# A fused attention and feed-forward kernel: the first block's attention by head halves, narrow dummy matmuls, and m-tiles in column pieces

## Chip, cores and metric

The kernel runs on one core of one Trainium2 chip. The metric is the device time of one execution in microseconds (us). Besides the timed runs there is one profiled execution, from which all views of the trace come.

## The reference

For each of 8 batches and 8 heads, a sequence of 576 tokens is cut into 9 chunks of 64 tokens, and softmax attention is done inside each chunk (head dimension 64). The heads are put side by side, which gives x of 4608 x 512, and x goes through a feed-forward layer with 2048 inner features and a swish with one beta per feature.

```python
def _attn_ref(q, k, v):                      # q, k, v: 8, 8, 576, 64
    scores = scale * np.matmul(q_c, k_c.transpose(0, 1, 2, 4, 3))   # chunks of 64
    scores = scores - np.max(scores, axis=-1, keepdims=True)
    attn = np.exp(scores)
    attn = attn / (np.sum(attn, axis=-1, keepdims=True) + 1e-09)
    return np.matmul(attn, v_c)

def _moe_ref(x, w_in, w_out, beta):          # x: 4608, 512
    h = x @ w_in                             # 512 x 2048
    g = h * (1.0 / (1.0 + np.exp(-beta * h)))
    return g @ w_out                         # 2048 x 512
```

## The kernel before

**Blocks.** The 4608 tokens are cut into nine blocks of 512 (`BLK`). Each block goes through attention (scores, exponential, P·V, normalization, transpose to the tile `xt`), then through L1 (x times w_in, silu, giving the tile `gt`) and L2 (`gt` times w_out, stored). L1 of a block is 16 m-tiles of 128 inner features; an m-tile is four matmuls of 128x128x512 (one for each quarter n of the 512 model columns) in one PSUM tile `hps`. From block 2 on, and in L2 from block 1 on, fewer products are used, with sums and differences of the operands; block 0 uses the plain products (`L1_first`, `L2_plain`). The code writes the order of all work by hand; each engine runs its instructions in that order. The waits between engines follow from the tiles that are read and written.

**Attention.** A group g is four chunks of all eight heads, i a pair of chunks: a block of 512 tokens has two groups and four pairs. The heads come in two halves, z = 0 and 1, of four heads each. q and k of a batch are loaded as two such halves for batch 0 (`split=True`), and each half is transposed on VectorE (`emit_T`, L135). `emit_sc(g)` makes the scores of both halves (L167) in a pair of PSUM tiles (`sc0` and `sc1`, or two of the pool `ps_p`, or the tile `x`) and then exponentials on ScalarE (L176). `emit_pv(i)` multiplies by V (L197); V has a column of ones, so that the sum of the exponentials comes with it. VectorE divides (a reciprocal and a multiplication, L209 to L214), once for the whole tile where the target is `x`, or once for each of two tiles. `emit_xp(i)` transposes the pair on TensorE (L232) and a copy on ScalarE or VectorE brings 128 columns of `xt` to SBUF.

**The head.** TensorE starts with 14 dummy matmuls on zeros, 512 columns wide (`emit_idle`, L244; their result is not read). Then come, in TensorE's order: half 0 of the scores of group 0, ten dummies, half 1 of group 0 and all of group 1, six dummies, P·V of pairs 0 and 1, four dummies, the transpose of pair 0, P·V of pair 2, two dummies, and `L1_first`. `L1_first` works the first four m-tiles in parts of 128 columns, each as soon as the columns of `xt` and the part of w_in are there, first with n = 0 and 2 (half 0 of the heads), then with n = 1 and 3. The m-tiles 4 to 15 follow at full width (`emit_m`).

**Loads.** POOL issues the loads of the inputs in a fixed order: q and k of batch 0 by halves, V of batch 0 in four loads (two for each half of the heads), w_in in five, w_out 0 to 7 in two, q and k of batch 1, w_out 8 to 11, V of batch 1 in four, w_out 12 to 15 in two, q and k of batch 2. beta comes over SP's queue. w_out is scaled by 1/beta (`binv`) after it has landed, on VectorE or ScalarE (`scale_w_out`, L122 and L126).

**L2 of block 0.** `L2_plain(0)` is a list of 20 units; a unit takes rows kk of w_out for one quarter t of the block: units 0 to 7 take kk 0 to 7, units 8 to 11 kk 8 to 11, units 12 to 15 kk 12 and 13, units 16 to 19 kk 14 and 15. Ahead of some units, hooks do the attention of block 1: scores of groups 2 and 3 ahead of unit 8, `emit_pv(4)` ahead of unit 11, `emit_pv(5)` ahead of unit 12, and so on. Block 1's L1 (`L1_plain`) already does its first five m-tiles in pieces of 128 columns and the sixth in two of 256.

Of the kernel before, what the change touches and what calls it, by code (L numbers as in the profile page):

```python
# [8 lines left out]
FP32 = mybir.dt.float32  # L9
FP16 = mybir.dt.float16  # L10
ACTF = mybir.ActivationFunctionType
ALU = mybir.AluOpType
# [3 lines left out]
def kernel(  # L16
# [74 lines left out]
                    in_=src[b].rearrange("(z a) (t r) d -> (a t) z (r d)", z=2, r=RUN)[:, zs],  # L91
                )

    def load_v(b):
        t = vbuf[b % NV]
        for z in range(2):
            for hp in range(2):
                h0 = 4 * z + 2 * hp
                nc.gpsimd.dma_start(  # L99
                    out=t[64 * hp:64 * hp + 64, 2 * z:2 * z + 2, :, 0:D].rearrange(  # L100
                        "p s c d -> p (s c) d"),
                    in_=v[b, h0:h0 + 2].rearrange("s (c p) d -> p (s c) d", p=CH),
                )
# [39 lines left out]
        return [lambda z=z, w=w: emit_T(b, z, w) for z in range(2) for w in range(2)]  # L143

    et_t = {}

    def emit_sc(g, where="s", between=None):
        if where == "x":
            scx = ps_x.tile([128, 2, 2, 4, CH], FP32, tag="x", name="scx")
            sc = [scx[:, 0], scx[:, 1]]  # L150
        else:
            sc = [
                ps_p.tile([128, 2, 4, CH], FP32, tag="p", name=f"scp{s}") if where == "p"
                else ps_s.tile([128, 2, 4, CH], FP32, tag=f"sc{s}", name=f"sc{s}")
                for s in range(2)
            ]
        for z in range(2):
            if z and between:
                between()
            for c in range(4):  # L160
                b, cb = divmod(4 * g + c, NCB)
                for e in range(2):
                    for a in range(4):
                        p0, o0 = 32 * a, 64 * (a // 2)
                        kk = kT[b][p0:p0 + 32, z].rearrange("p t r e -> p (t r) e")
                        qq = qT[b][p0:p0 + 32, z].rearrange("p t r e -> p (t r) e")
                        nc.tensor.matmul(  # L167
                            out=sc[a % 2][o0:o0 + 64, z, c, :],
                            lhsT=kk[:, cb * CH:(cb + 1) * CH, e],
                            rhs=qq[:, cb * CH:(cb + 1) * CH, e],  # L170
                            start=(e == 0),
                            stop=(e == 1),
                        )
        et = et_t[g] = et_p.tile([128, 2, 2, 4, CH], FP16, tag="et", name="et")
        for o, i_ in [(et, scx)] if where == "x" else [(et[:, s], sc[s]) for s in range(2)]:
            nc.scalar.activation(out=o, in_=i_, func=ACTF.Exp, scale=scale)  # L176

    xt_t = {}

    x16_t = {}  # L180

    def emit_pv(i, where="x", xbar=True):
        g = i // 2
        spare = where != "x"
        if where == "p":
            xs = [ps_p.tile([128, 4, 128], FP32, tag="p", name="xp") for _ in range(2)]
        elif where == "s":
            xs = [ps_s.tile([128, 4, 128], FP32, tag=f"sc{h}", name="xp") for h in range(2)]
        else:
            x = ps_x.tile([128, 2, 4, 128], FP32, tag="x", name="x")  # L190
            xs = [x[:, 0], x[:, 1]]
        for s in range(4):
            z, a2 = s // 2, s % 2
            for hp, cp in ((0, 0), (1, 1), (0, 1), (1, 0)):
                b, cb = divmod(2 * i + cp, NCB)
                p0, o0 = 64 * hp, 64 * cp
                nc.tensor.matmul(  # L197
                    out=xs[hp][o0:o0 + 64, s, 0:D + 1],
                    lhsT=et_t[g][p0:p0 + 64, a2, z, 2 * (i % 2) + cp, :],
                    rhs=vbuf[b % NV][p0:p0 + 64, s, cb, 0:D + 1],  # L200
                )
        rd = rd_p.tile([128, 2, 4, 1], FP32, tag="rd", name="rd")
        x16 = x_p.tile([128, 2, 4, D], FP16, tag="x16", name="x16")
        for xx, rr, yy in (
            [(xs[h], rd[:, h], x16[:, h]) for h in range(2)] if spare else [(x, rd, x16)]
        ):
            shape = [128] + list(yy.shape[1:])
            if spare:
                nc.vector.reciprocal(out=rr, in_=xx[:, :, D:D + 1])  # L209
                src = xx[:, :, 0:D]  # L210
            else:
                nc.vector.reciprocal(out=rr, in_=xx[:, :, :, D:D + 1])
                src = xx[:, :, :, 0:D]
            nc.vector.tensor_tensor(  # L214
                out=yy, in0=src, in1=rr.to_broadcast(shape), op=ALU.mult,
            )
        j, t0 = i // 4, (i % 4) * 128
        if j not in xt_t:
            xt_t[j] = xt_p.tile([128, KDM, BLK], FP16, tag="xt", name="xt")
        xf = x16.rearrange("p e s d -> p (e s d)")  # L220
# [33 lines left out]
    def emit_h(j, m, c0=0, c1=BLK, ns=range(KDM)):  # L254
        if (j, m) not in hps_t:
            hps_t[j, m] = ps_p.tile([128, BLK], FP32, tag="p", name="hps")
        for n in ns:
            e, z = n // 2, n % 2
            nc.tensor.matmul(  # L259
                out=hps_t[j, m][:, c0:c1],  # L260
                lhsT=w_r[m // 4][:, 2 * z + e, m // 2 % 2, m % 2, :],
                rhs=xt_t[j][:, n, c0:c1],
                start=(n == 0 and c0 == 0),
                stop=(n == KDM - 1),
                skip_group_check=True,
            )
# [86 lines left out]
        for i in range(2):  # L353
            silu(m2 + i, dn_, sb["t"][:, i])

    def emit_m(j, m):
        emit_h(j, m)
        emit_g(j, m)

    HT = BLK // 2  # L360
# [178 lines left out]
    def dve(n=1):  # L539
        for _ in range(n):  # L540
            if fill:
                fill.pop(0)()

    def L1_first():
        gt_t[0] = gt_p.tile([128, KFF, BLK], FP16, tag="gt", name="gt")

        def part(t, ns, m_last=False):
            for m in range(4):
                emit_h(0, m, t * 128, (t + 1) * 128, ns)
                if m_last:  # L550
                    emit_g(0, m)

        emit_xp(1)
        part(0, (0, 2))
        part(1, (0, 2))
        emit_pv(3, xbar=False)
        emit_xp(2)
        part(0, (1, 3))
        part(1, (1, 3))
        emit_xp(3, eng=nc.vector)  # L560
        table(ACTF.Silu)
        part(2, (0, 2, 1, 3))
        part(3, (0, 2, 1, 3), True)
        for m in range(4, 6):
            hps_t[0, m] = ps_s.tile([128, BLK], FP32, tag=f"sc{m % 2}", name="hps")
        for m in range(4, KFF):
            emit_m(0, m)

    def L1_plain(j, hooks, pieces={}):
        gt_t[j] = gt_p.tile([128, KFF, BLK], FP16, tag="gt", name="gt")  # L570
        for m in range(KFF):
            hooks.get(m, lambda: None)()
            w = BLK // pieces.get(m, 1)
            for c in range(0, BLK, w):
                emit_h(j, m, c, c + w)
            emit_g(j, m)
# [32 lines left out]
    with tc.manual_schedule():  # L609
# [24 lines left out]
        load_w_out(7, 1)  # L634
        load_qk(2)

        emit_idle(14)
        for f in T_items(0):
            f()
        nc.vector.transpose(  # L640
# [6 lines left out]
        nc.vector.scalar_tensor_tensor(  # L647
            out=beta2, in0=bt, scalar=eps, in1=bm, op0=ALU.subtract, op1=ALU.mult)
        nc.vector.tensor_scalar_add(beta2, beta2, eps)
        nc.vector.reciprocal(out=binv, in_=beta2)  # L650
        emit_sc(0, between=lambda: emit_idle(10))
        emit_sc(1, where="p")
        emit_idle(6)
        emit_pv(0, xbar=False)
        emit_pv(1, where="s", xbar=False)
        d = emit_idle(4)
        emit_xp(0, "p")
        emit_pv(2, xbar=False)
        emit_idle(2, d=d)

        L1_first()
        emit_sw()
        scale_w_out(range(0, 4))
        scale_w_out(range(4, 8))
# [132 lines left out]
```

## Time and profile before

| | us |
|---|---|
| five timed runs, median | 278.06 |
| lowest and highest | 277.27, 278.15 |
| profiled execution, its own time | 278.28 |
| span of the profile, first to last instruction | 276.5 |

| engine | busy us (share of the span) |
|---|---|
| PE (TensorE matmul) | 267.7 (97%) |
| PEld (weight load) | 192.4 (70%) |
| DVE (VectorE) | 215.5 (78%) |
| ACT (ScalarE) | 163.3 (59%) |
| POOL (GpSimd) | 95.6 (35%) |

Where the first stages lie, by the timeline: first dummies from 1.19 to 6.24; first scores at 8.91; first P·V at 15.23; first m-tile matmul at 18.23; the last m-tiles of block 0 end and the first `ops` matmul of L2 follows at 33.69; the first m-tile of block 1 begins at 51.38.

A line of the timeline has the start in us, the time in us, the engine, the line of code, the operation, what it writes and reads, the shape, the number of instructions merged in it and, in brackets, the engine's idle time ahead of it with what ended it. Matmuls are pipelined, so that the duration of one (0.38 us for 512 columns) is longer than the distance from one to the next. In a row of windows, each engine's busy time has its number of instructions behind it; then come the granted clock of TensorE as a fraction of full speed, the share of the DMA engines and the GB/s.

### The profile page before, as it was taken

How to read it: one execution, taken by the hardware profiler on the slowest of the kernel's cores; microseconds unless marked ns; L12 is line 12 of the kernel's file. 1: busy time of each engine (PE TensorE's matmuls, PEld its weight loads, DVE VectorE, ACT ScalarE, POOL GpSimd, SP SyncE). 2: the span in 40 equal slices, each digit the busy share in tenths (PEclk: the TensorE clock that was granted, in tenths of full speed). 3: DMA queues.
4: the chain of work that ended last, by engine and by line, in shares of the span. 5: the costliest groups of instructions: out<-in, count | busy, mean ns of one | idle time of the engine just before them, and what ended most of it. 6: DMA issues, size and time to landing. Idle time of an engine off the chain costs nothing.

```text
span 276.5 us, 8403 instructions
## 1 busy us (share of the span) xinstructions
PE 267.7 (97%) x3612; PEld 192.4 (70%) x3612; DVE 215.5 (78%) x428; ACT 163.3 (59%) x276; POOL 95.6 (35%) x106
## 2 busy tenths in 40 slices
PE   7799999999999999999999999999999999999994
PEld 2356444756886688668866886688668866887684
DVE  2744664888688899889988988898679867996854
ACT  2049736878256854785478547853784478316820
POOL 8733445162107820782078204820311031013100
PEclk9799999999999999999999999999999999999999
DMA  6999999999946964797479342924202320232013
GB/s 100 172 200 211 211 180 207 186 261 197 89 117 138 178 59 116 134 179 63 116 149 176 49 116 79 87 42 116 78 0 59 100 76 0 60 98 76 0 40 115
DMA packets 69654, 32.01 MB, mean 116 GB/s; under 512 B 53745, under 2 KB 63985, under 8 KB 69617
## 3 DMA queue, kind: packets, MB, share of 16 engines
q0 software_dynamic: 45024, 18.35, 55.4%
q1 hardware_dynamic: 24448, 12.99, 17.9%
q8 instruction: 28, 0.46, 0.7%
q10 hardware_dynamic: 144, 0.13, 0.1%
q14 instruction: 10, 0.07, 0.1%
HBM read 36.71 MB, written 9.44 MB: 167 GB/s over the span
## 4 chain that ended last, share of the span: by engine, by line
PE 88%; DMA 5%; DVE 3%; POOL 2%; issue 1%; ACT 0%; DVEq 0%; ACTq 0%; POOLq 0%
PE hps L259 27%; PE oA L414 19%; PE wA L313 9%; PE wX L313 6%; PE oB L414 5%; PE oD L414 5%; PE ops L513 5%; PE oC L414 4%; DMA vb<-in_v_dram 3%; PE x L197 2%; PE scx L167 2%; PE sc L167 2%; DMA xt<-x 2%; PE xps L232 1%; POOL vb L99 1%
## 5 line engine op out<-in xcount | busy, mean ns | idle before, releaser
L259 PE MATMUL hps<-xt,wi 128*128 128x512 f16 (+2 forms) x464 | 85.2, 328 | 0.6 <-issue 0.5
L270 ACT ACTIVATE gt<-hps,beta 128x512 f16<-128x512 f32 x88 | 57.8, 683 | 21.0 <-PE hps L259 20.9
L259 PEld LDWEIGHTS <-wi 128*128 128x128 f16 x464 | 39.4, 98 | 27.1 <-issue 0.7
L414 PEld LDWEIGHTS <-s 128*128 128x128 f16 x496 | 47.6, 98 | 6.2 <-DVE s L374 0.5
L414 PE MATMUL oA<-tw,s 128*128 128x256 f16 x368 | 44.3, 273 | 0.0
L414 PEld LDWEIGHTS <-gt 128*128 128x128 f16 x384 | 36.3, 98 | 6.6
L425 ACT COPY u<-oA 128x512 f32<-128x512 f32 x24 | 14.1, 586 | 41.9 <-PE oA L414 41.9
L321 DVE COPY u<-wA 128x512 f32<-128x512 f32 x42 | 28.6, 682 | 5.0 <-PE wA L313 5.0
L99 POOL DMA_DIRECT2D vb<-in_v_dram x32 | 27.4, 874 | 7.0 <-DMA w_out<-in_moe_w_out_dram 3.2
L344 POOL TENSOR_TENSOR t<-u,w 128x512 f32<-128x512 f32 x14 | 17.8, 1274 | 33.6 <-DVE u L321 33.6
L313 PEld LDWEIGHTS <-sw 128*128 128x128 f16 x224 | 21.9, 98 | 9.5 <-issue 0.8
L483 POOL TENSOR_TENSOR o<-t,o 128x512 f32<-128x512 f32 x7 | 8.9, 1271 | 51.7 <-ACT o L480 42.7
L452 POOL TENSOR_TENSOR w<-u,u 128x512 f32<-128x512 f32 x7 | 9.9, 1412 | 47.2 <-ACT u L425 25.9
L135 DVE STREAM_TRANSPOSE qT<-qu 128x576 f32<-128x576 f32 x16 | 20.0, 1250 | 4.3 <-DMA qu<-in_q_dram 4.2
L135 DVE STREAM_TRANSPOSE kT<-ku 128x576 f32<-128x576 f32 x16 | 19.9, 1244 | 3.7 <-DMA ku<-in_k_dram 3.5
L313 PEld LDWEIGHTS <-wi 128*128 128x128 f16 x168 | 16.4, 98 | 4.9
L607 ACT ACT_TABLE_LOAD x15 | 19.2, 1283 | 0.3
L324 ACT ACTIVATE gt<-c,beta 128x512 f16<-128x512 f32 x28 | 18.7, 716 | 0.2
L372 DVE TENSOR_TENSOR s<-gt 128x512 f16<-128x512 f16 x32 | 17.8, 556 | 0.0
L313 PE MATMUL wA<-xs,sw 128*128 128x256 f16 x112 | 16.8, 273 | 0.6 <-DVE u L321 0.6
L374 DVE TENSOR_TENSOR s<-s,gt 128x512 f16<-128x512 f16 x32 | 15.6, 488 | 1.1
L176 ACT ACTIVATE et<-sc 128x512 f16<-128x512 f32 x18 | 9.7, 596 | 11.1 <-PE sc L167 11.1
(87 smaller groups left out, 407.2 us busy)
## 6 DMA issues: line engine op xcount, KB each, us to landing
out_dram<-osb SPq DMA_DIRECT2D x21, 256.0 KB, 3.6
vb<-in_v_dram POOLq DMA_DIRECT2D x32, 144.0 KB, 8.4
out_dram<-o SPq DMA_DIRECT2D x14, 256.0 KB, 2.2
qu<-in_q_dram POOLq DMA_DIRECT2D x6, 576.0 KB, 7.9
ku<-in_k_dram POOLq DMA_DIRECT2D x6, 576.0 KB, 10.7
wi<-in_moe_w_in_dram POOLq DMA_DIRECT2D x3, 512.0 KB, 12.1
w_out<-in_moe_w_out_dram POOLq DMA_DIRECT2D x3, 512.0 KB, 15.6
qu<-in_q_dram POOLq DMA_DIRECT2D x4, 288.0 KB, 11.3
```

Source lines behind the costliest of these rows:

```text
L99: nc.gpsimd.dma_start(out=t[64 * hp:64 * hp + 64, 2 * z:2 * z + 2, :, 0:D].rearrange("p s c d -> p (s c) d"), in_=v[b, h0:h0 + 2].rearrang ...
L135: nc.vector.transpose(out=dst[b][:, z].rearrange("p t r e -> p (t r e)").bitcast(FP32).rearrange("p (t r) -> p r t", r=RUN), in_=src[b][:, ...
L259: nc.tensor.matmul(out=hps_t[j, m][:, c0:c1], lhsT=w_r[m // 4][:, 2 * z + e, m // 2 % 2, m % 2, :], rhs=xt_t[j][:, n, c0:c1], start=(n == ...
L270: nc.scalar.activation(out=gt_t[j][:, m, :], in_=hps, func=ACTF.Silu, scale=beta2[:, m % 2, m // 2:m // 2 + 1],)
L313: nc.tensor.matmul(out=bank[b][:, i, :], lhsT=a[:, kk, q, i, :], rhs=rhs[:, kk, :], start=(first and i == 0 and kk == 0), stop=(kk == 1), ...
L321: nc.vector.tensor_copy(out=sb[nm], in_=bank[b])
L324: nc.scalar.activation(out=gt_t[j][:, m, cols], in_=src, func=ACTF.Silu, scale=beta2[:, m % 2, m // 2:m // 2 + 1],)
L344: nc.gpsimd.tensor_tensor(out=sb["t"], in0=sb["u3"], in1=sb["w1"], op=ALU.add)
L372: tt(out=s1[:, lo], in0=g[:, lo, dn], in1=g[:, hi, dn], op=ALU.add)
L374: tt(out=s2[:, lo], in0=s1[:, lo], in1=g[:, lo, up], op=ALU.subtract)
L414: nc.tensor.matmul(out=bank[name][:, i, :], lhsT=a[:, kk, i * 128:(i + 1) * 128], rhs=b[:, kk, :], start=(first and i == 0 and n == 0), st ...
L607: nc.scalar.activation(out=warm2, in_=warm, func=func, scale=1.0)
```

## The change

The change does several things at once.

- The first 14 wide dummies become 88 of 32 columns and 10 of 512.
- In the head, the two groups are no longer done one after the other, but the halves of the heads are: scores and exponentials of half 0 for both groups (`head_sc(0)`), seven dummies, half 1 for both groups. P·V (`head_pv`) and the transpose (`head_xp`) work on one group and one half at a time, so that a transposed piece holds 256 columns of two quarters n instead of 128 columns of four. The dummies between are 7, 1, 3 and 1 instead of 10, 6, 4 and 2.
- `L1_first` takes the first four m-tiles in four parts of 256 columns and two n each.
- The m-tiles 4 to 11 of block 0 are done in four pieces of 128 columns.
- The reciprocal for `binv` stands after `L1_first` in VectorE's order.
- `load_v` gets a parameter that no call uses; the normalization moves to a function `normed` without change; `sc_part` is the inner part of the old `emit_sc`.

```diff
+    def sc_part(g, z, sc):
+        for c in range(4):
+            b, cb = divmod(4 * g + c, NCB)
+            for e in range(2):
+                for a in range(4):
...
+                    nc.tensor.matmul(
+                        out=sc[a % 2][o0:o0 + 64, z, c, :],
+                        lhsT=kk[:, cb * CH:(cb + 1) * CH, e],
+                        rhs=qq[:, cb * CH:(cb + 1) * CH, e],
...
-    def emit_m(j, m):
-        emit_h(j, m)
+    def emit_m(j, m, pieces=1):
+        w = BLK // pieces
+        for c in range(0, BLK, w):
+            emit_h(j, m, c, c + w)
         emit_g(j, m)
...
+    def head_sc(z):
+        if z == 0:
+            for g in range(2):
+                sc_h[g] = [
+                    ps_s.tile([128, 2, 4, CH], FP32, tag=f"sc{s}", name=f"sc{s}") if g == 0
+                    else ps_p.tile([128, 2, 4, CH], FP32, tag="p", name=f"scp{s}")
+                    for s in range(2)
+                ]
+                et_t[g] = et_p.tile([128, 2, 2, 4, CH], FP16, tag="et", name="et")
+        for g in range(2):
+            sc_part(g, z, sc_h[g])
+            for s in range(2):
+                nc.scalar.activation(
+                    out=et_t[g][:, s, z], in_=sc_h[g][s][:, z], func=ACTF.Exp, scale=scale)
+
+    def head_pv(g, z, where="x"):
+        if where == "s":
+            xs = [ps_s.tile([128, 4, 128], FP32, tag=f"sc{h}", name="xp") for h in range(2)]
+        else:
+            x = ps_x.tile([128, 2, 4, 128], FP32, tag="x", name="x")
+            xs = [x[:, 0], x[:, 1]]
+        for ti in range(2):
+            for a2 in range(2):
+                for hp, cp in ((0, 0), (1, 1), (0, 1), (1, 0)):
+                    c = 2 * ti + cp
+                    p0, o0 = 64 * hp, 64 * cp
+                    nc.tensor.matmul(
+                        out=xs[hp][o0:o0 + 64, 2 * ti + a2, 0:D + 1],
+                        lhsT=et_t[g][p0:p0 + 64, a2, z, c, :],
+                        rhs=vbuf[0][p0:p0 + 64, 2 * z + a2, 4 * g + c, 0:D + 1],
+                    )
+        x16_t[g, z] = normed(xs, None if where == "s" else x)
+
+    def head_xp(g, z, where, eng=None):
+        xf = x16_t.pop((g, z))
...
+        for kk in range(KDM):
+            nc.tensor.transpose(
+                out=xps[:, kk, :], in_=xf[:, kk * 128:(kk + 1) * 128], identity=ident
+            )
+        dst = xt_t[0].rearrange("p (e z) (i c) -> p z e i c", z=2, c=128)[:, z, :, 2 * g:2 * g + 2]
+        src = xps.rearrange("p (e i) c -> p e i c", e=2)
+        if eng:
+            eng.tensor_copy(out=dst, in_=src)
+        else:
+            nc.scalar.copy(out=dst, in_=src)
...
     def L1_first():
...
-        def part(t, ns, m_last=False):
+        def part(g, z):
             for m in range(4):
-                emit_h(0, m, t * 128, (t + 1) * 128, ns)
-                if m_last:
+                emit_h(0, m, g * 256, (g + 1) * 256, (z, 2 + z))
+                if (g, z) == (1, 1):
                     emit_g(0, m)
 
-        emit_xp(1)
-        part(0, (0, 2))
-        part(1, (0, 2))
-        emit_pv(3, xbar=False)
-        emit_xp(2)
-        part(0, (1, 3))
-        part(1, (1, 3))
-        emit_xp(3, eng=nc.vector)
+        part(0, 0)
+        head_xp(0, 1, "x")
         table(ACTF.Silu)
-        part(2, (0, 2, 1, 3))
-        part(3, (0, 2, 1, 3), True)
+        part(1, 0)
+        head_xp(1, 1, "s1", eng=nc.vector)
+        part(0, 1)
+        part(1, 1)
...
         for m in range(4, KFF):
-            emit_m(0, m)
+            emit_m(0, m, 4 if m < 12 else 1)
...
-        emit_idle(14)
+        d = emit_idle(88, w=32)
+        emit_idle(10, d=d)
...
+        head_sc(0)
+        d = emit_idle(7)
+        head_sc(1)
+        emit_idle(1, d=d)
+        head_pv(0, 0)
+        head_pv(1, 0, "s")
+        emit_idle(3, d=d)
+        head_xp(0, 0, "p")
+        head_pv(0, 1)
+        emit_idle(1, d=d)
+        head_xp(1, 0, "p")
+        head_pv(1, 1, "s")
+
+        L1_first()
         nc.vector.reciprocal(out=binv, in_=beta2)
-        emit_sc(0, between=lambda: emit_idle(10))
-        emit_sc(1, where="p")
-        emit_idle(6)
-        emit_pv(0, xbar=False)
-        emit_pv(1, where="s", xbar=False)
-        d = emit_idle(4)
-        emit_xp(0, "p")
-        emit_pv(2, xbar=False)
-        emit_idle(2, d=d)
-
-        L1_first()
```

More of the change, by code (lines that the diff above doesn't have):

```diff
@@ L92, in load_qk, with load_v @@
                 )
-    def load_v(b):
+    def load_v(b, zs=(0, 1)):
         t = vbuf[b % NV]
-        for z in range(2):
+        for z in zs:
             for hp in range(2):
@@ L145, with emit_sc @@
     et_t = {}
-    def emit_sc(g, where="s", between=None):
+    sc_h = {}
+    def sc_part(g, z, sc):
[3 more added lines that the diff above has]
+                for a in range(4):
+                    p0, o0 = 32 * a, 64 * (a // 2)
+                    kk = kT[b][p0:p0 + 32, z].rearrange("p t r e -> p (t r) e")
+                    qq = qT[b][p0:p0 + 32, z].rearrange("p t r e -> p (t r) e")
+                    nc.tensor.matmul(
+                        out=sc[a % 2][o0:o0 + 64, z, c, :],
+                        lhsT=kk[:, cb * CH:(cb + 1) * CH, e],
+                        rhs=qq[:, cb * CH:(cb + 1) * CH, e],
+                        start=(e == 0),
+                        stop=(e == 1),
+                    )
+    def emit_sc(g, where="s"):
         if where == "x":
@@ L157, in emit_sc @@
         for z in range(2):
[L158 to L173, printed above, removed]
+            sc_part(g, z, sc)
         et = et_t[g] = et_p.tile([128, 2, 2, 4, CH], FP16, tag="et", name="et")
@@ L180, with normed @@
     x16_t = {}
+    def normed(xs, x=None):
+        rd = rd_p.tile([128, 2, 4, 1], FP32, tag="rd", name="rd")
+        x16 = x_p.tile([128, 2, 4, D], FP16, tag="x16", name="x16")
+        for xx, rr, yy in (
+            [(x, rd, x16)] if x is not None else [(xs[h], rd[:, h], x16[:, h]) for h in range(2)]
+        ):
+            nc.vector.reciprocal(out=rr, in_=xx[..., D:D + 1])
+            nc.vector.tensor_tensor(
+                out=yy, in0=xx[..., 0:D], in1=rr.to_broadcast([128] + list(yy.shape[1:])),
+                op=ALU.mult,
+            )
+        return x16.rearrange("p e s d -> p (e s d)")
     def emit_pv(i, where="x", xbar=True):
@@ L201, in emit_pv @@
                 )
[L202 to L216, printed above, removed]
+        xf = normed(xs, None if spare else x)
         j, t0 = i // 4, (i % 4) * 128
@@ L219, in emit_pv @@
             xt_t[j] = xt_p.tile([128, KDM, BLK], FP16, tag="xt", name="xt")
-        xf = x16.rearrange("p e s d -> p (e s d)")
         if xbar:
@@ new lines, in head_pv @@
+    def head_pv(g, z, where="x"):
[13 more added lines that the diff above has]
+                        rhs=vbuf[0][p0:p0 + 64, 2 * z + a2, 4 * g + c, 0:D + 1],
+                    )
+        x16_t[g, z] = normed(xs, None if where == "s" else x)
@@ new lines, in head_xp @@
+    def head_xp(g, z, where, eng=None):
+        xf = x16_t.pop((g, z))
+        if 0 not in xt_t:
+            xt_t[0] = xt_p.tile([128, KDM, BLK], FP16, tag="xt", name="xt")
+        pool, tag = {"x": (ps_x, "x"), "s1": (ps_s, "sc1"), "p": (ps_p, "p")}[where]
+        xps = pool.tile([128, KDM, 128], FP16, tag=tag, name="xps")
+        for kk in range(KDM):
+            nc.tensor.transpose(
+                out=xps[:, kk, :], in_=xf[:, kk * 128:(kk + 1) * 128], identity=ident
+            )
+        dst = xt_t[0].rearrange("p (e z) (i c) -> p z e i c", z=2, c=128)[:, z, :, 2 * g:2 * g + 2]
[4 more added lines that the diff above has]
+            nc.scalar.copy(out=dst, in_=src)
@@ L572, in L1_plain @@
             hooks.get(m, lambda: None)()
[L573 to L576, printed above, removed]
+            emit_m(j, m, pieces.get(m, 1))
             if m == 8:
```

## The prediction

> **What bounds the kernel now.** First the page's slices, to see which engine is full and where it is not.
>
> ```profile
> PE   7799999999999999999999999999999999999994
> PEclk9799999999999999999999999999999999999999
> DMA  6999999999946964797479342924202320232013
> ```
>
> TensorE (PE) is full from the third slice (6.9 us each) on; only the first two slices, where the change works, have holes, and there the clock is once below full. The DMA row matters as much: from slice 2 to slice 9 (7 to 62 us) the transfer engines are full too. So PE sets the end, but for the first 60 us it consumes data that arrive at a pace of their own.
>
> Next the chain of waits, in order of time, for the head and what follows (start, us, what).
>
> ```profile
> 6.10 9.47 DMA vb<-in_v_dram
> 15.62 0.25 PE x L197 x7
> ...
> 21.71 12.15 PE hps L259 x80
> 33.85 6.91 PE ops L513 x32
> ...
> 41.96 2.70 PE ops L513 x12
> 44.65 0.36 PE x L197 x16
> ...
> 51.54 1.79 PE hps L259 x32
> ```
>
> The head hangs on the fourth V load of batch 0, landed at 15.57: the 9th matmul of the first P·V group waits for it. From 21.71 on it is PE without a break. The last line gives a price: 32 matmuls of 128 columns in 1.79 us, 56 ns each, weight loads hidden.
>
> Then the granted clock, by short windows (us; PE, PEld, DVE, ACT, POOL busy, clock, DMA share, GB/s).
>
> ```profile
> 8.30:8.40 0.10, 0.00 (x0) 0.00 (x0) 0.10 (x1) 0.00 (x0) 0.10 (x1) 0.93 0.97 184
> 8.40:8.50 0.10, 0.00 (x0) 0.00 (x0) 0.10 (x1) 0.00 (x0) 0.10 (x1) 0.50 1.47 277
> ...
> 11.70:11.80 0.10, 0.10 (x2) 0.04 (x1) 0.10 (x1) 0.00 (x0) 0.10 (x1) 0.51 2.37 151
> 11.80:11.90 0.10, 0.10 (x1) 0.00 (x0) 0.10 (x1) 0.00 (x0) 0.10 (x1) 1.00 2.41 152
> ```
>
> The clock drops at about 8.39 and returns at 11.80; dummies start 0.427 us apart until 5.0 and 0.216 after (the record shows 1.00 before 5.0 too). So its changes lie about 3.4 us apart: 5.0, 8.4, 11.8. PE idled from 6.24 to 8.91, waiting for kT.
>
> Last the transfers behind the second attention block, by the issue's timeline and the time to landing.
>
> ```profile
> 32.70 0.85 POOL L99 DMA_DIRECT2D vb<-in_v_dram  x1 [0.55 <-DMA qu<-in_q_dram]
> vb<-in_v_dram POOLq DMA_DIRECT2D x1, 144.0 KB, 11.1
> ...
> 39.20 1.33 ACT L122 ACTIVATE w_out<-w_out,binv 128x512 f16<-128x512 f16 x2 [4.63 <-DMA w_out<-in_moe_w_out_dram]
> 44.59 0.32 PE L197 MATMUL x<-vb,et 64*64 64x65 f16 x16
> ```
>
> The fourth V load of batch 1 lands at 32.70 + 11.1 = 43.8; the group that reads it (`emit_pv(4)`) starts at 44.59. That is under 1 us of slack, and the issue itself waited for an earlier transfer, not for PE.
>
> **The change, part by part.**
>
> *First dummies.* 14 wide (1.19 to 6.24) become 88 narrow and 10 wide. No row shows a narrow one. From below: 32/512 of a wide one, 27 ns at half clock and 13 at full. From above, an estimate: a weight load that isn't hidden, as long as a 128-column pass, 107 ns at half clock. I take the nearest row, 56 ns (the same 128x128 load with 128 columns): 88 x 0.056 = 4.9, to 6.1; ten wide at 0.216 = 2.2, to 8.3. The scores wait for kT, half 0, until 8.87 anyway (transpose 7.60 + 1.26), so the dummies cost nothing unless they end after it, and PE may now hold full clock there.
>
> *Scores by halves.* Half 0 of both groups (64 matmuls) at 8.9: before, 32 took 0.57 us at half clock and 96 took 0.96 at full, so 0.64 to 1.15. Seven wide dummies add 1.5 (full) to about 2.6 (clock back at 11.8): PE is free between 11.1 and 12.6, kT half 1 is there at 12.15 (10.89 + 1.26). Before, ten dummies held PE until 12.87. Half 1 is done at 12.9 to 13.3. The four exponentials of 128x512 at 0.60 become eight of 128x256. Nearest row: the 128x256 silus, 0.47. That is 1.4 us more on ACT, but half the eight run before 12.2, and group 0's half 1 ends near 13.7.
>
> *P·V by halves.* Half 0 needs only the first two V loads (3.55 + 8.1 = 11.7 and 4.41 + 8.3 = 12.7). Both groups of half 0 run by 14.0; VectorE normalizes them (0.90 in one piece, 1.2 in two) by 15.8; one transpose and its copy (0.59) fit too. Half 1 still waits until 15.6. Then come its matmuls (0.25), a dummy 0.2, a transpose 0.25 and the other P·V 0.25: 16.6. Counts of P·V matmuls, transposes and copies are the same; one normalization is split, +0.3 on VectorE. `binv` (0.55) leaves its place ahead of them. Its readers wait for w_out until 28.5.
>
> *First m-tiles.* 32 matmuls of 256 columns at 0.109 (16 in 1.75 in the chain) = 3.5, against 64 of 128 at 0.056 = 3.6: equal. They are placed by transfers: w_in's first half lands at 7.55 + 9.3 = 16.85, its second at 8.28 + 10.7 = 19.0. So part(0,0) 17.0 to 17.9, transpose, part(1,0) to 19.0, transpose, part(0,1) to 20.1, part(1,1) to 21.0. The next block of w_in lands at 9.31 + 11.4 = 20.7, just in time. Before, m-tile 4 started at 23.5 (33.86 less 12 x 0.864). Gain there: 2.5 us.
>
> *Pieces.* Eight m-tiles take 16 x 0.056 = 0.90 instead of 4 x 0.216 = 0.864: +0.25 in all. Here the Trainium skill speaks against the change: "TensorE: Matmul & The Clock Gate", Back-to-back issue gap, gives about 81 ns a matmul at 128 columns with weight loads. By it the 128 matmuls cost 3.2 us more and the head's gain is gone. The trace's 32 in 1.79 us decides: 56. L2 then starts at 21.0 + 7.2 + 3.5 = 31.6 instead of 33.7: 2.1 us gained.
>
> *What is late next.* Units 0 to 7 of `L2_plain(0)` (6.9) find w_out scaled: four blocks by 30.0, four by 32.5. Scores 2 and 3 then run from 38.4 to 39.7, kT being ready at 37.9. Unit 8 needs w_out 8 to 11, which land at 39.13; ACT ends scaling the second at 40.53, so PE waits about 0.9 and the twelve matmuls end near 43.0, 1.5 ahead of before. Then `emit_pv(4)` runs into the V load: its tenth matmul goes at about 43.85 instead of 44.67. **Gain 0.8; of the 2.1, 1.3 is waited away.** No load moves: POOL's issue order is untouched, SP issues nothing between the beta loads and the first store at 50.7, PE's progress triggers no load in this stretch, and POOL's issues waited for transfers. I cost their shift at nothing; each microsecond by which that V load moved would move this bound by as much.
>
> *From there on.* w_out 12 to 15 land at 44.2 and 45.5, scaled in time for 45.7 and 48.6. VectorE's next hold, k of batch 3 at 46.03 + 17.3 = 63.3, stays fixed. Its queue behind that ends at 70.66, PE's next P·V shifts from 70.42 to 69.6, so that normalization gains only 0.2, but the next (74.77) has 1.9 us of idle ahead of it and takes the full 0.8; so do the transposed x (landed 81.3) and L1(2) behind it. After that PE is full. Sum: profiled execution 278.28 (span 276.5, 1.8 around it) less 0.8 = 277.5; the median of the five runs, 278.06, is 0.2 lower, so 277.3.
>
> **The clock, weighed.** The same page (Why this matters for your kernels) asks for no idle gap above about 3 us; by it no gap here, all about 1 us or less, costs anything. The row is stricter: a gap of 2.7 us lost the clock, with 64% of that 3.4 us window idle; 0.55 us idle of 3.3 (18.2 to 21.5, 17%) kept it. The new waits make about 32% idle in 11.8 to 15.2 and 26 to 30% in the two windows after 39.1. I take 0, since 32% is nearer to 17; the other end is a window at half clock, up to 1.7.
>
> **The rivals.**
>
> *Kept whole (8%).* The V load doesn't hold PE, and 2.1 arrive: 276.0. For it: landing is read to 0.1 us and DMA could be quicker. Against it: full DMA slices up to 62 us.
>
> *Given back (13%).* VectorE is nearly without idle from 63.4 to 70.7; if normalization or the transposed x doesn't follow, 0.3 or less stays: about 277.9, which is no change.
>
> *The clock is lost at the new waits (21%).* PE pauses about 0.9 us at 39.7 and 0.8 at 43.0. If a third of a window idle is enough, the next 3.4 us of L2 run at half clock with no wait to hide it: +1.7 - 0.8 = +0.9, 279.0. It decides where the idle share that drops the clock lies below about 30%; shown are only 17% (kept) and 64% (lost). For it: nothing in the trace lies between. In the head the same loss would mostly be eaten by the 1.3 us to spare. The dummies belong to the same question: at 107 ns, all at half clock, they end at 1.2 + 9.4 + 4.3 = 14.9, six microseconds late, and the head would end 2.2 later than before; it breaks even near 90 ns.
>
> **How the numbers follow.** The cap by the V load has 58%: 277.3, its own range 276.9 to 277.8. The measurement can tell about 0.2% (0.56 us); of the 58, 8 fall within it. Faster 50 + 8 = 58%, the same 8 + 13 = 21%, slower 21%. The range 276.4 to 279.0 takes in the cap, the giving back and half of the lost clock; the best case and the rest are left out.
>
> **What would show it.** Right: PE at m-tile 4 near 21; ops starting near 31.6; a PE wait before unit 8 on w_out and one of about 0.8 inside `emit_pv(4)` on vb; everything from 45 to the end 0.8 earlier. Wrong: first scores after 10; granted clock 0.50 anywhere after 12; L2 starting after 33; vb of batch 1 landing away from 43.8; or a new wait on VectorE between 70 and 85.

## The result and the profile after

The changed kernel takes 276.96 us (median of 44 runs; 275.47 to 278.8) against 277.67 us for the kernel before (median of 79 runs). The ratio is 0.9977, with a 95% interval of 0.9967 to 0.9987: 0.7 us less, where 0.8 was forecast. The profiled execution of the changed kernel took 277.72 us, with a span of 275.9. It lies 0.8 above its median, as the one before lay 0.6 above its own, so the two profiles can be set side by side. Each is one execution only; e12 below has a second one of the changed kernel, which took 276.71.

First the slices, as they were shown of before:

```profile
PE   8699999999989999999999999999999999999994
PEclk9799999999999999999999999999999999999999
DMA  6999999999977944894489242924202320332013
```

PE's second slice still holds the wait for the first scores, and the clock still drops there. The DMA row is full to slice 9 as before: up to there the data arrive at much the same pace.

Then the chain of waits (start, us, what), the stretch in which the prediction looked for the cap:

```profile
11.54 11.67 DMA wi<-in_moe_w_in_dram
23.21 0.28 issue
23.49 15.43 DMA w_out<-in_moe_w_out_dram
...
39.00 1.34 ACT w_out L122 x2
40.35 0.04 issue
40.39 2.53 PE ops L515 x11
42.92 0.21 PE x L212 x9
43.13 0.03 issue
43.16 0.30 PE x L212 x7
...
49.98 1.79 PE hps L259 x32
```

Before, this chain was PE's from 21.71 on. Now it runs over transfers until 39: w_in, then w_out 8 to 11, then its scaling on ACT, then PE. The P·V group is cut after its ninth matmul (42.92, nine; 43.16, seven), as predicted: the tenth needs the fourth V load of batch 1. That load landed sooner than in the profile of before, by the issue's timeline and its time to landing (32.41 + 10.7 = 43.1, before 43.8):

```profile
32.41 0.85 POOL L99 DMA_DIRECT2D vb<-in_v_dram  x1 [0.55 <-DMA qu<-in_q_dram]
vb<-in_v_dram POOLq DMA_DIRECT2D x1, 144.0 KB, 10.7
```

The landmarks in the timelines of the two profiles, in us:

| | before | changed | gain |
|---|---|---|---|
| first m-tile matmul | 18.23 | 16.95 | 1.3 |
| first `ops` matmul of L2 | 33.69 | 31.50 | 2.2 |
| `ops` after the first P·V of block 1 | 44.84 | 43.35 | 1.5 |
| first m-tile of block 1 | 51.38 | 49.82 | 1.6 |
| first product of block 2's L1 (`wA`) | 81.67 | 80.05 | 1.6 |
| second set of products in `wA` | 84.22 | 82.97 | 1.25 |
| last products (`oCi`) | 271.08 | 270.27 | 0.8 |

Of 2.2 us at the start of L2, 0.7 is waited away near 40 us: 0.4 ahead of the second matmul of unit 8 (the first starts at 39.78, the second at 40.39, and without a wait they lie 0.22 apart) and 0.25 inside the P·V group (0.50 from its start to the next `ops`, where it was 0.25). More goes later. The timelines show how, first the changed kernel's, then the line of before:

```profile
80.17 0.42 DVE L293 TENSOR_TENSOR xs<-xt 128x512 f16<-128x512 f16 x1 [1.22 <-DMA xt<-x]
82.97 0.60 PE L313 MATMUL wA<-xs,sw 128*128 128x256 f16 x4 [1.02 <-DVE u L321]
```

```profile
84.22 0.60 PE L313 MATMUL wA<-xs,sw 128*128 128x256 f16 x4 [0.65 <-DVE u L321]
```

VectorE waits 1.22 us for the transposed x of block 2, and the copy of `wA` that PE needs stands behind its four `xs` sums. PE waits 1.02 there; before it waited 0.65.

### The profile page after: what moved, and what is told of

Same layout as the page of the kernel before. It is cut to its first block, busy times and chain, and to the rows that moved or that the text cites. A ratio compares the mean times of both kernels' runs of the same rounds, so it can differ in the third digit from the quotient of the medians.

```text
span 275.9 us, 8684 instructions
## 1 busy us (share of the span) xinstructions
PE 266.7 (97%) x3750; PEld 197.3 (71%) x3750; DVE 215.4 (78%) x430; ACT 163.7 (59%) x280; POOL 95.6 (35%) x106
## 4 chain that ended last, share of the span: by engine, by line
PE 78%; DMA 14%; DVE 4%; issue 1%; ACT 1%; POOL 1%; DVEq 0%; ACTq 0%; POOLq 0%
PE hps L259 22%; PE oA L416 19%; PE wA L313 9%; PE wX L313 6%; DMA w_out<-in_moe_w_out_dram 6%; PE oB L416 5%; PE oD L416 5%; DMA wi<-in_moe_w_in_dram 4%; PE oC L416 4%; DMA ku<-in_k_dram 3%; PE ops L515 2%; PE x L212 2%; DMA xt<-x 1%; PE sc L156 1%; PE scx L156 1%
## 5 line engine op out<-in xcount | busy, mean ns | idle before, releaser
L259 PEld LDWEIGHTS <-wi 128*128 128x128 f16 x528 | 42.8, 98 | 22.9
L485 POOL TENSOR_TENSOR o<-t,o 128x512 f32<-128x512 f32 x7 | 8.9, 1271 | 53.1 <-ACT o L482 43.8
L313 PEld LDWEIGHTS <-wi 128*128 128x128 f16 x168 | 16.4, 98 | 4.9
L324 ACT ACTIVATE gt<-c,beta 128x512 f16<-128x512 f32 x28 | 18.7, 716 | 0.3
L313 PE MATMUL wA<-xs,sw 128*128 128x256 f16 x112 | 16.8, 272 | 1.4 <-DVE u L321 1.4
L156 PEld LDWEIGHTS <-kT 32*64 32x64 f16 x1152 | 11.4, 107 | 5.7 <-DVE kT L135 2.9
```

Source lines behind the costliest of these rows:

```text
L156: nc.tensor.matmul(out=sc[a % 2][o0:o0 + 64, z, c, :], lhsT=kk[:, cb * CH:(cb + 1) * CH, e], rhs=qq[:, cb * CH:(cb + 1) * CH, e], start=(e ...
L259: nc.tensor.matmul(out=hps_t[j, m][:, c0:c1], lhsT=w_r[m // 4][:, 2 * z + e, m // 2 % 2, m % 2, :], rhs=xt_t[j][:, n, c0:c1], start=(n == ...
L313: nc.tensor.matmul(out=bank[b][:, i, :], lhsT=a[:, kk, q, i, :], rhs=rhs[:, kk, :], start=(first and i == 0 and kk == 0), stop=(kk == 1), ...
L324: nc.scalar.activation(out=gt_t[j][:, m, cols], in_=src, func=ACTF.Silu, scale=beta2[:, m % 2, m // 2:m // 2 + 1],)
```

## The experiments

All ratios are to the kernel before on the same chip, with 95% intervals. Two questions were open: whether the data near 40 us cap the gain (theory A, against B, where PE's own work sets the pace), and what the 128-column pieces are for, since the prediction costed them at 0.25 us lost.

**e1: no pieces.**

```diff
-            emit_m(0, m, 4 if m < 12 else 1)
+            emit_m(0, m)
```

> The changed kernel with m-tiles 4 to 11 at full width again. Theory A (arrival of data sets the pace near 40 us): L2 starts about 0.25 us earlier, near 31.25, the waits ahead of unit 8 and inside the first P.V group of block 1 grow by as much, and the whole stays as in the changed kernel, 0.7 us under the kernel before (within 0.2). Theory B (TensorE's own work sets the pace): 0.25 us faster than the changed kernel, 0.95 under the kernel before. Theory C (the pieces themselves bring the gain): no gain is left, or less than 0.3 us.

Measured: 278.99 us, ratio 1.0043 (1.0021 to 1.0065), slower than the kernel before. So one line of the change, which only cuts matmuls smaller, is worth 1.8 us (1.0043 against 0.9977), and neither A nor B says why. Its profiled execution took 282.42, the longest of its twelve, so only the kind of wait is taken from it, not the size; e10 below has the same wait at the same place in an execution below its own median. TensorE's waits and its timeline in e1:

```profile
PE oA L416 <- issue: 2.0, 1, 2.0
...
70.08 0.30 PE L212 MATMUL xp<-vb,et 64*64 64x65 f16 x16
70.31 0.28 PE L416 MATMUL oA<-tw,s 128*128 128x256 f16 x1
72.64 2.74 PE L416 MATMUL oA<-tw,s 128*128 128x256 f16 x12 [2.05 <-issue]
```

TensorE stops inside a run of equal matmuls, after the first of sixteen. "Issue" is the page's word for a wait that it can put down to nothing. But the page lists a queue of its own kind, q8 "instruction", 28 packets, 0.46 MB: 16 KB each. And the view of transfers has exactly one of them in the half microsecond from 69.5 to 70.0, just ahead of the stop:

```profile
q8 instruction: 1, 0.02, 15.9%
```

**Theory D** came from this: TensorE's instructions arrive in blocks of 16 KB over the same transfer engines as the data, and it stands still when it has used up one block before the next has landed. The pieces and the narrow dummies then matter by the number of instructions they put into the stream.

**e2 and e7: dummies added to the head** (5 or 12 wide ones).

```diff
         head_pv(1, 1, "s")
+        emit_idle(5, d=d)
```

> The changed kernel with five wide dummies (5 x 0.216 = 1.08 us) put behind the last P.V of the head, ahead of the first m-tile. Theory A: L2 starts near 32.6 instead of 31.5, the waits for data swallow the delay, and the whole is as in the changed kernel, 0.7 us under before (0.4 to 0.9). Theory B: the delay counts in full, 0.4 us slower than the kernel before.

Measured: 276.84 us, 0.9967 (0.9949 to 0.9985). A microsecond of extra work in the head costs nothing that can be measured; B, which had 0.4 over before, falls. The profile shows why:

```profile
38.94 0.71 PE L156 MATMUL scx<-qT,kT 32*64 32x64 f16 x64
42.84 0.32 PE L212 MATMUL x<-vb,et 64*64 64x65 f16 x16
```

From the scores to P·V are 3.90 us, as in the kernel before (40.69 to 44.59), where the changed kernel took 4.35 (38.50 to 42.85): the waits near 40 us are gone, and P·V starts no later than in that profile without the dummies.

> The changed kernel with twelve wide dummies (2.6 us) behind the last P.V of the head. Theory A (1.3 to 1.5 us of the head's gain is waited away for data near 40 us): L2 starts near 34.1, and 1.1 to 1.3 us of the 2.6 come through: 0.4 to 0.7 us slower than the kernel before. Theory B (no slack): 1.9 slower than before.

Measured: 278.37 us, 1.0028 (1.0004 to 1.0052), 0.8 us over before (278.37 is 0.57 over that chip's median of 277.80; the ratio of runs gives 0.0028 x 277.8 = 0.8). Against the changed kernel's 0.9977 that is 1.4 us lost of 2.6 added: about 1.2 us of the head's gain are spare, give or take 0.7 by e7's interval.

**e3 and e4: 0.5 MB less to load**, in the changed kernel and in the one before.

```diff
+        nc.vector.memset(w_out16[:, 2:4], 0.0)
...
-        load_w_out(2)
```

> The changed kernel without the load of w_out rows 512 to 1023 (zeros instead, 0.5 MB less to move before 28 us); the output is therefore not the reference's. Theory A: every later load lands about 2.5 us earlier, TensorE no longer waits ahead of unit 8 or in the P.V group, and the gain of 2.2 at L2's start reaches 45 us: 1.2 to 2.2 us under the kernel before. Theory B: as the changed kernel, 0.7 under.

> The kernel before without the same load (zeros instead; the output is not the reference's). Theory A: before, TensorE did not wait for data after 20 us, so nothing is gained up to 66 us: within 0.2 us of the kernel before. Rival: if data arriving earlier help later stages in any case (VectorE's hold for k of batch 3, the transposed x), it is 0.3 to 1 us faster as well, and the difference to the changed kernel with less data is what the change is worth without that cap.

Measured: 276.23 us, 0.9947 (0.9922 to 0.9971), and 277.77 us, 0.999 (0.9974 to 1.0006). With less data the change is worth 0.43% (1.2 us) instead of 0.23%, as A has it, but neither step is clear of noise: e4's interval takes in 1, and e3's overlaps with that of the changed kernel. The profile of e3 bears out one half of A. ACT begins to scale w_out 8 to 11 at 36.4 instead of 39.0, and from the scores (39.38) to P·V (43.28) it is again 3.90 us, without a wait. The other half, that the gain then reaches 45 us, it doesn't show: this execution lost its clock in the head (0.62 granted from 13 to 16 us, 0.50 from 16 to 17), L2 started at 32.38, 0.9 later than in the changed kernel, and the `ops` after P·V came at 43.53, not earlier than its 43.35.

**e5: no pieces, 96 more narrow dummies at the start.**

```diff
-        d = emit_idle(88, w=32)
+        d = emit_idle(184, w=32)
```

> The changed kernel without pieces, but with 184 narrow dummies instead of 88 at the start, so that TensorE's stream has as many instructions ahead of m-tile 12 as in the changed kernel (96 pairs of weight load and matmul moved). Theory D (the pieces only shift where the 16 KB blocks of TensorE's instruction stream begin, 256 instructions each; without them a block is asked for too late near 70 us and TensorE stands still for 2 us): the stall is gone and the time is as in the changed kernel, 0.7 us under before (0.3 to 1.2). Theory C (full-width m-tiles are slower in themselves, by pace or by colliding with transfers): as without pieces, 1.2 us over before.

Measured: 279.73 us, 1.006 (1.0039 to 1.0082): D's forecast failed, and it is at least as slow as C said. But its profile has no stop near 70 us. It stops twice in the head instead:

```profile
8.89 0.44 PE L156 MATMUL sc<-qT,kT 32*64 32x64 f16 x29
10.62 0.22 PE L156 MATMUL sc<-qT,kT 32*64 32x64 f16 x3 [1.30 <-issue]
...
14.53 0.30 PE L572 MATMUL xp<-vb,et 64*64 64x65 f16 x5
17.37 0.35 PE L572 MATMUL xp<-vb,et 64*64 64x65 f16 x11 [2.54 <-issue]
```

The count speaks for D all the same. The first stop comes after 194 dummies and 29 score matmuls, 223 in all. The second comes after 194 + 64 + 7 + 64 + 1 + 16 + 5 = 351, which is 128 later. 128 pairs of weight load and matmul are 256 instructions; if one block holds them, each has 64 of its 16,384 bytes.

**e6: the pieces alone in the kernel before** (the same loop in `emit_m`'s place).

```diff
-            emit_m(0, m)
+            w = BLK // (4 if m < 12 else 1)
+            for c in range(0, BLK, w):
+                emit_h(0, m, c, c + w)
+            emit_g(0, m)
```

> The kernel before with m-tiles 4 to 11 of block 0 in four pieces of 128 columns and nothing else. By cost alone (8 x 0.03 us): 0.25 us slower than before. Theory C (pieces help in themselves): 1 us faster or more. Theory D: the 192 more instructions move the block borders; where they land at a dense stretch of small matmuls it is 1 to 3 us slower, else 0.25 slower.

Measured: 279.11 us, 1.0039 (1.0018 to 1.006). Its waits show 0.9 us on issue at an `oA` matmul (67.3 us) and 0.3 in the scores at 78.2. The pieces help one kernel and hurt the other: C falls.

**e8: the dummies' order turned round**, 14 wide first and then 84 narrow, as many as in the changed kernel.

```diff
-        d = emit_idle(88, w=32)
-        emit_idle(10, d=d)
+        d = emit_idle(14)
+        emit_idle(84, w=32, d=d)
```

> The changed kernel with 14 wide and then 84 narrow dummies at the start, instead of 88 narrow and 10 wide: the same number of instructions. Theory A and D: the first scores wait for kT either way and the block borders are the same: as the changed kernel, 0.7 us under before (0.3 to 1.1). Rival (the order holds the clock at the first scores, and that matters): 0.3 us or more off the changed kernel.

Measured: 278.6 us, 1.0025 (1.0005 to 1.0045). The expectation of A and D failed. The rival said that there would be a difference, but not for the right reason: the clock was held (1.00 from 6 to 23 us in e8's profile), and the kernel is slower. The timeline:

```profile
1.19 8.25 PE L244 MATMUL idle<-zero 128*128 128x512 f16 x98 [1.19 <-DVE zero L656]
...
12.24 0.35 PE L156 MATMUL scp<-qT,kT 32*64 32x64 f16 x22
14.92 0.28 PE L156 MATMUL scp<-qT,kT 32*64 32x64 f16 x10 [2.33 <-issue]
```

98 + 64 + 7 + 54 = 223 matmuls again. The number of instructions is that of the changed kernel, which passes its 223rd matmul at 13.5 without a stop; what differs is when the dummies were through. This execution, 277.52, is among the shortest of e8 and shows the kind of the loss; that the stop is the whole of the 1.3 us between the two ratios is not shown. Ten of the twelve runs list a mean clock of 0.995 or less, and this one does not: most of them lost clock as well. That sharpened D: the place of a border is a matter of counting, but whether the block is there is a matter of when it is asked for.

**e9: no pieces, 96 narrow dummies where the pieces were.**

```diff
+        emit_idle(96, w=32, d=hps_t[0, 4])
         for m in range(4, KFF):
-            emit_m(0, m, 4 if m < 12 else 1)
+            emit_m(0, m)
```

> The changed kernel without pieces, with 96 narrow dummies put between m-tile 3 and m-tile 4 instead: as many instructions as the pieces add, at the place where they were, with nothing moved in the head. Theory D (late blocks of TensorE's instruction stream): no wait on issue in the head and none near 70 us; the dummies cost 1.3 to 2.6 us, of which 1.1 to 1.3 is covered by the wait for data near 40 us, so 0.7 us under before to 0.5 over. Theory C (full-width m-tiles are slower in themselves): no better than without pieces, 1.2 us over before or more.

Measured: 278.32 us, 1.0026 (1.0008 to 1.0043), a little over D's range in the median (0.7 over before, 0.5 allowed). TensorE's list of waits has no line with issue in it. The dummies are the price, by the timeline:

```profile
20.82 2.55 PE L244 MATMUL hps<-zero 128*128 128x32 f16 x96
```

2.4 us until the next matmul, less 0.25 for the pieces saved: 2.2 us later at L2, and by e7's slack of 1.2 about 1.0 of it comes through. That makes 0.4 over before; 0.7 was measured. C wanted 1.2 or more, which is the very end of the interval. By time alone e9 doesn't differ clearly from e1 (1.0043); it is the missing stop that speaks for full-width m-tiles having no fault of their own.

**e10 and e11: the first dummies exchanged alone**, the old ones in the changed kernel and the new ones in the kernel before.

> The changed kernel with the old 14 wide dummies at the start and no narrow ones: 168 instructions fewer. Theory A alone (data): kT sets the first scores, so as the changed kernel, 0.7 us under before. Theory D: the first block is asked for during the second half of the scores, while the V loads fill the transfer engines, and TensorE waits on issue 0.5 to 2.5 us in the head; the borders after it move too: 0 to 2 us over before.

> The kernel before with 88 narrow and 10 wide dummies in place of the first 14 and nothing else. Theory D: the first block is asked for near 7 us, ahead of the V loads' crowd, and the 0.5 us wait on issue at 18.6 us goes; near 70 us the border lies elsewhere (168 instructions on), which may bring a wait there. 0.5 us under before if not, up to 1.5 over if so. Theory A alone: no change, within 0.2 us.

Measured: 281.0 us, 1.0123 (1.0092 to 1.0154), and 281.27 us, 1.0156 (1.0122 to 1.019). Both ranges were too low; the signs are D's. A alone, with 0.7 under and no change, is out by more than 3 us. The largest stops, first of e10 (a third, of 0.45, lies at 46.0) and then of e11:

```profile
16.75 0.31 PE L572 MATMUL xp<-vb,et 64*64 64x65 f16 x13
18.26 0.22 PE L572 MATMUL xp<-vb,et 64*64 64x65 f16 x3 [1.21 <-issue]
...
70.50 0.23 PE L212 MATMUL xp<-vb,et 64*64 64x65 f16 x5
72.69 0.28 PE L212 MATMUL xp<-vb,et 64*64 64x65 f16 x11 [1.97 <-issue]
```

```profile
68.43 0.82 PE L414 MATMUL oB<-w_out,gt 128*128 128x256 f16 x6
72.20 1.25 PE L414 MATMUL oB<-w_out,gt 128*128 128x256 f16 x10 [2.95 <-issue]
```

e11 did lose the 0.55 us wait in the head, as expected, and got 2.95 near 70 us.

**e12: the changed kernel again**, on the chip of e9 to e11.

> The changed kernel unaltered, beside the other three on one chip. 0.7 us under before (0.4 to 1.0), no wait on issue of 0.3 us or more on TensorE in its profile.

Measured: 276.82 us, 0.9974 (0.9955 to 0.9993). No wait on issue on TensorE; 0.5 for V in the head, 0.2 for the scaled w_out at 40, 0.9 of 1.1 for VectorE at 82. Its first `ops` came at 31.10, the `ops` after P·V at 42.76, the last products at 269.29: 1.8 us ahead of before, where the first profile of the same kernel had 0.8.

**Counted over all of them.** The matmuls ahead of a border, the start of the matmul at the border before (128 earlier), the start of the 16 KB packet on q8, and the stop, all from the traces. The twelve stops are all waits on issue above 0.15 us that TensorE has in the 14 profiles:

| kernel | matmuls before it | border before | packet starts | stands still |
|---|---|---|---|---|
| before | 223 | 13.2 | 16.8 | 18.6 to 19.1 |
| e4 | 223 | 13.1 | 16.3 | 18.2 to 18.7 |
| changed | 223 | 6.1 | 7.0 | no (13.5) |
| e5 | 223 | 3.8 | 8.2 | 9.3 to 10.6 |
| e8 | 223 | 9.2 | 12.5 | 12.6 to 14.9 |
| e10 | 223 | 12.2 | 15.9 | 17.1 to 18.3 |
| e5 | 351 | 10.6 | 15.2 | 14.8 to 17.4 |
| e10 | 607 | 40.3 | 43.8 | 45.6 to 46.0 |
| e6 | 990 | 64.9 | 65.7 | 67.3 to 68.2 |
| e11 | 990 | 65.7 | 69.8 | 69.3 to 72.2 |
| e1 | 991 | 65.7 | 69.9 | 70.6 to 72.6 |
| e10 | 991 | 66.0 | 70.1 | 70.7 to 72.7 |
| changed | 991 | 57.3 | 57.6 | no (64.9) |
| changed | 1119 | 64.9 | 68.8 | no (72.8) |
| e6 | 1246 | 76.1 | 76.0 | 78.2 to 78.6 |

Nine stops lie on 223 plus a multiple of 128; three, in e6 and e11, lie one matmul earlier, and why is not shown. From the packet's start to the next matmul it takes 2.2 to 2.7 us at every stop. The other borders agree: of the first nine in each of the 14 profiles (126), none is passed less than 2.2 us after its packet started. So TensorE stops where it has used up its block before that time is over.

The packet itself starts at very different times after the border before: 0.3 and 0.9 us in the changed kernel (57.3, 6.1), 3.2 to 4.5 us in the head of the kernels that stop there (3.8 to 13.2) and mostly about 4 near 66, but 0.8 in e6. A crowd of other transfers is the obvious reason, but the share of the DMA engines doesn't show it. These are the two microseconds around 6.1, 57.3 and 64.9 in the changed kernel, where the packet came 0.9, 0.3 and 3.9 us after the border:

```profile
5.10:7.10 2.00, 1.83 (x7) 0.57 (x5) 1.25 (x1) 0.00 (x0) 2.00 (x4) 1.00 1.10 196
56.30:58.30 2.00, 2.00 (x11) 0.88 (x9) 2.00 (x3) 1.55 (x3) 2.00 (x3) 1.00 1.09 260
63.90:65.90 2.00, 2.00 (x136) 1.74 (x135) 1.97 (x6) 1.80 (x3) 0.00 (x0) 1.00 1.09 207
```

The share is 1.1 in all three. Where the packet is late, the two times add up to an estimate of about 6 us (3.2 to 4.5 and 2.2 to 2.7): a block that is used up faster makes TensorE stop. Scores use up their pairs at 10 ns each or less (64 in 0.64 us by the chain of before), P·V at 16 (16 in 0.25).

Here the Trainium skill bears on the case. "Runtime: NRT & Kernel Launch", section Instruction fetch mechanics, describes such blocks of 16 KiB, fetched over a queue of the sequencer's own, and calls their cost mostly hidden. The size agrees with q8's packets (0.46 MB in 28). Hidden it is not in e11, where TensorE stands still for 2.95 us at one of them; here the measurement decides.

## Why the prediction was right, and where not

**The total** (277.3 on the five runs' median, 0.8 gained): 0.7 measured. The cap by arriving data is real: PE waits for w_out 8 to 11 and for V where the prediction put them, and e2 shows that a microsecond of the head is spare. That the number was hit so closely is in part luck, as two errors of about 0.7 us cancel.

**The head** came out by its sum: first m-tile 16.95 (17.0 forecast), L2 at 31.50 (31.6), scores of block 1 at 38.50 (38.4), the twelve matmuls of units 8 to 10 done at 42.9 (43.0). One reading was off by one: in the first P·V group of batch 0 the chain has seven matmuls left, so it is the tenth that waits for the fourth V load, not the ninth.

**The cap's size** was off, and the error was made good by another. The prediction had waits of 0.9 and 0.8 us; they were 0.4 and 0.25. It held the V load at 43.8; it landed at 43.1 in the changed kernel's profile, so the gain past it was 1.5 instead of 0.8. "No load moves" was a step that failed; from execution to execution the loads do (this V load was issued at 32.70 before, 32.41 in the changed kernel, 32.06 in e2). Then the step "PE is full after that" failed: between 80 and 84 us 0.4 goes to VectorE's wait for the transposed x, and 0.4 near 194 us to another wait for VectorE (0.39 for `u`). The wait near 82 is in e12 too (0.93), the one near 194 is not, so the second is no fixed cost. The rival that let VectorE give gains back was right in kind, and partly came true. Three of the signs that the prediction named for being wrong did show, each small: half clock past 12 us, V away from 43.8, and a longer wait for VectorE between 70 and 85.

**The narrow dummies**: 56 ns each was chosen, between 27 and 107. They took 27 (89 in 2.41 us by the windows below), the low end, and 25 in e9 at full clock (96 in 2.4 us). That moved no time by itself, since kT comes later. The break-even near 90 ns doesn't follow from the prediction's own figures either: 2.2 us over 88 dummies are 25 ns each, so 82. But the whole step was thought of as filling TensorE's wait. What it does besides is to get through a border early: without it, or with the order turned round, TensorE stops in the head (e10, e8).

**The clock** was not lost at the new waits (1.00 from 31.5 to 46.0 in the windows of the changed kernel), so that rival fell. In this execution it was lost in the head, where the prediction hoped to keep it: at half speed from 9.3 to 12.5.

```profile
1.19:3.60 2.41, 2.41 (x89) 2.41 (x90) 0.29 (x5) 1.03 (x2) 2.35 (x5) 1.00 0.39 58
...
9.30:9.40 0.10, 0.03 (x4) 0.03 (x4) 0.02 (x1) 0.00 (x0) 0.00 (x0) 0.50 1.67 195
...
31.50:46.00 14.50, 14.14 (x225) 6.79 (x227) 9.71 (x15) 6.99 (x12) 8.23 (x12) 1.00 1.47 195
```

But that is a matter of the execution, not of the kernel. In e12, the same kernel, it was kept:

```profile
9.00:12.00 3.00, 2.35 (x71) 1.23 (x71) 2.44 (x3) 1.21 (x4) 1.56 (x3) 1.00 2.08 152
12.00:16.00 4.00, 3.33 (x122) 2.04 (x123) 3.12 (x13) 1.80 (x5) 2.38 (x4) 1.00 1.65 186
```

The timed runs list each one's mean granted clock, and the two profiles compared above, which both have a stretch of 3.4 us at half speed, have 0.993 and 0.994. Of the changed kernel's 44 runs, 12 are at 0.995 or less, with a median of 277.5 against 276.7 for the rest; of the 86 runs of the kernel before that are listed beside the experiments, 39, with 278.15 against 277.4. So a lost clock goes with about 0.8 us more in these lists (the twelve runs of e12, three of them lost, don't show it), and the change gains about 0.7 with it and without.

**The pieces**: the sum's term (+0.03 us a tile) was right as a cost, and the 56 ns a matmul hold (32 in 1.79 at 49.98 above). What was missing is that every instruction added or removed moves the borders of all blocks behind it. No step of the prediction looked at the instruction queue, although the page of before lists q8 and its timeline has a stop:

```profile
18.23 0.33 PE L259 MATMUL hps<-xt,wi 128*128 128x128 f16 x3
19.11 0.90 PE L259 MATMUL hps<-xt,wi 128*128 128x128 f16 x13 [0.55 <-issue]
```

14 + 32 + 10 + 96 + 6 + 32 + 4 + 4 + 16 + 2 + 4 + 3 = 223 matmuls. The prediction read these 0.55 us only as idle time for the clock. The chain of waits of before has them on it (18.56, 0.55, issue), so they are a part of the 2.2 us that L2 starts earlier. The other kernels of this study show that the same edits cost 1 to 4 us when one of them is made alone or left out (e6, e11, e1, e10). That they bring a gain together rests on borders that happen to fall well; the prediction had no term for that, and that it came out is luck as well.

**Still open**: why e9 lies 0.3 us higher than a slack of 1.2 makes it (its interval holds both), why the packet starts 0.3 us after the border at one place and 4 at another, and whether another number of dummies would do better. No experiment separates the transposed x near 82 us from what delays it.

## What to carry to other kernels

Where TensorE waits on "issue" in the middle of equal matmuls, count its instructions: if the stops lie a fixed number apart (128 here) and a packet of the instruction queue starts shortly before TensorE goes on, it is short of instructions, not of data. Stretches of many small matmuls are the place to look, and any edit that changes the number of instructions ahead of them, dummies and tile sizes too, has to be measured for that side effect. One profile is one execution: the same kernel kept its clock in one and lost it in the other. And a gain at the head is worth only what the next arrival of data leaves of it: add dummies until the time moves, and the slack is known.

## What was not expected of the hardware

- TensorE's stops fall on multiples of 128 matmul pairs, to within one, and at such a border it stands still for 0.35 to 2.95 us.
- A stop can cost the clock too, and its length alone doesn't decide it: after 2.54 us in e5 the granted clock was 0.53 from 17.4 to 21.0; after 2.33 in e8, 1.97 in e10 and 2.95 in e11 it stayed at 1.00.
- A 128x128 weight load with a 32-column matmul takes 25 ns at full clock (e9) and 27 in the first 2.4 us of the changed kernel, where the wide dummies that follow still start 0.43 us apart, twice their 0.216 at full clock.
